# Operand differences as steps of their own, and output-weight sums of three pairs without a trip through DRAM, in attention with two split-fp32 MLPs

## The chip, the cores and the metric

One of the eight cores of a Trainium2 chip runs the kernel. TensorE (PE in the profile) multiplies, with its weight loads shown apart (PEld); VectorE (DVE), ScalarE (ACT) and GpSimd (POOL) work on tiles; SyncE (SP) issues all transfers between DRAM and the on-chip memory. The metric is device microseconds (us) of one execution, the median over several runs.

## What is computed

Attention with a causal window of 128 and a linear position bias, for 4 batches and 8 heads of 576 positions by 64, then two MLPs of 512 to 2048 to 512 over the 2304 positions. The weights of the MLPs reach the chip as 64-bit floats. The reference, cut to what matters:

```python
scores = scale * np.matmul(q, k.transpose(0, 1, 3, 2))
...
attn = attn / (np.sum(attn, axis=-1, keepdims=True) + 1e-09)
x = np.matmul(attn, v)                      # (2304, 512), float32

h = x @ w_in;  r = np.maximum(h, 0.0)       # first MLP
x = (s * (r * r) + b) @ w_out
h = np.maximum(x @ moe2_w_in, 0.0)          # second MLP
out = h * h @ moe2_w_out
```

## The kernel before

**Split products.** Every float32 operand is kept as a high part in the narrow type fp32r and a low part that holds the rest. ACT makes the high part by a copy, DVE the low part by a subtraction (`split`). A product is three matmuls: high by high, high by low, low by high.

**Weights.** A 64-bit word becomes a float32 in steps: a load (token `l`), a first step on ACT and DVE (`a`), a second on ACT or DVE and then POOL or DVE (`b`), and the split into halves (`c`), which are stored to DRAM (`d`) and loaded when they are used (`w`). The words of the second MLP are loaded into three buffers named `st`, for one pair of 128-row blocks of the hidden dimension at a time, eight pairs in all (0 to 7).

**The second MLP's first layer** (phases 0 to 3, each over a quarter of the positions, 32 token numbers in all) uses seven products instead of eight for a 2x2 block product (`p`, 6 matmuls of 128x384 each, out to the PSUM banks `px` and `py`). `m`, `u`, `v` copy partial results to the temps m1, u2, u3 (tiles `tm`, `tu`, `r_all`), `j` adds such a temp to a bank and ACT takes the relu, `r` squares.

**The second MLP's second layer** in phases 0 and 1 is plain (`F`). In phases 2 and 3 it too takes seven products (m = 1, 2, 7, 6, 5, 4, 3, eight steps each, one per pair, so that step number e = 8 times the place of m, plus the pair). Its weight operands are sums and differences of blocks of w_out, which the steps `N` (sums, `second_sums`), `R` (halves) and `t` (stores to `we`) make once for each pair, and which `e` loads (256 KB each) into a ring of places. Its other operand comes from four results of the first layer, a11, a12, a21 and a22: for m = 7 it is a11 - a21, for m = 6 a21 + a22 - a11, for m = 3 a12 - a11, for the others one of the four. `second_operand` (token `g`) makes it: DVE the sum or difference, then ACT the high half, then DVE the low half. `second_product` (token `X`) multiplies, 9 matmuls of 128x256 into the bank `q`. The difference of m = 7 always goes to the one temp u3, which is the tile `r_all`; those of m = 6 and m = 3 overwrite the results (tiles `ywih`, `ywil`, `ywoh`, `ywol`, `yr`). The halves go to a ring of 6 places in phase 2 and 10 in phase 3 (names `m2...`, `sh`, `sl`).

**Output weights and DRAM.** The converted words of w_out of a pair are first split and stored as they are (`c`, `d`). The float words of all but pairs 0 and 1 are stored to DRAM as well (`x`, `store_words`, a transfer `wx<-st`) and come back (`y`, `load_words`, `st<-wx`) much later, when `N`, `R` and `t` make the sums.

**What sets the order.** A list of tokens, `ORDER`, is written out; each token issues its instructions at once, and every engine, and the queue of transfers on SP, executes its instructions in that order. A step that waits holds up everything behind it on its engine. `UNIT_ENGINES` and `CHOICE` say which engine takes the steps that more than one can do (`v` DVE, `g` POOL, `s` ACT). All instructions are issued through one helper, so the profile gives them all line 29 (L29).

Of the kernel before, what the change touches and what calls it, by code (L numbers as in the profile page):

```python
# [18 lines left out]
class InOrder:  # L19
# [20 lines left out]
    T4 a03 a01 c00 b03 b01 C2 U2 D7 X1 S5 c02 X2 X3 L0 i l10 P5 L1 C4 T5 G0 c01 a10 C5 G1 U4 L2 c03 H0 b10 U5 l12 H1 L3  # L40
    l11 D8 X4 D9 G2 G3 M0 X5 M1 H2 M2 a12 H3 S7 l13 a11 S6 c10 L4 b12 L5 b11 P7 P6 M3 T7 T6 c11 C7 C6 G4 U7 U6 L6 G5 c12
    L7 l20 H4 M4 a13 X6 H5 G6 S8 X7 L8 l22 b13 G7 P8 M5 L9 D10 T8 H6 H7 c13 G8 l21 a20 C8 l23 G9 L10 D11 M6 a22 U8 H8 X8
    L11 H9 S9 M7 b20 G10 M8 L12 P9 T9 G11 b22 L13 a21 C9 U9 H10 H11 M9 D12 X9 G12 S10 L14 b21 G13 M10 P10 M11 T10 H12
    H13 c21 L15 c20 M12 c22 C10 U10 G14 a23 H14 X10 l30 G15 M13 L16 S11 M14 b23 L17 G16 P11 D13 L18 T11 H15 c23 M15 H16
    C11 G17 l32 a30 G18 U11 H17 X11 H18 L19 G19 b30 L20 S12 M16 L21 k0.1 a32 l31 M17 M18 P12 T12 a31 H19 G20 c30 C12 H20
    L22 l33 G21 b32 U12 X12 L23 G22 H21 S13 L24 M19 a33 b31 M20 M21 H22 P13 l34 b33 T13 G23 C13 c31 a34 M22 H23 U13 L25
    c33 G24 G25 c32 L26 k3.0 D14 L27 H24 M23 H25 X13 D15 S14 G26 G27 M24 l35 b34 L28 L29 P14 k4.1 T14 M25 H26 a35 C14
    H27 c34 k4.0 G29 b35 U14 M26 D16 X14 G28 H28 S15 L30 c35 P15 M27 M28 T15 C15 D17 G30 L31 H29 G31 U15 X15 L32 S16 M29
    H30 H31 D18 G32 L33 P16 T16 M30 D19 C16 H32 G33 M31 M32 H33 S17 U16 L34 P17 T17 X16 G34 C17 M33 L35 H34 S18 U17 M34
    G35 X17 H35 P18 L36 D20 T18 G36 C18 M35 D21 S19 U18 L37 H36 P19 T19 X18 M36 C19 S20 D22 U19 G37 L38 H37 P20 M37 T20  # L50
    G38 X19 C20 L39 S21 U20 H38 G39 H39 L40 P21 M38 G40 L41 M39 D23 H40 T21 G41 L42 X20 H41 C21 k6.0 S22 U21 M40 k0.0
    P22 T22 X21 C22 M41 S23 U22 G42 D24 H42 k7.0 k1.1 L43 P23 T23 X22 M42 C23 S24 G43 H43 k3.1 U23 P24 L44 T24 D25 D26
    C24 X23 M43 k1.0 G44 H44 L45 G45 S25 U24 L46 D27 M44 k5.0 X24 P25 T25 H45 G46 k2.1 C25 H46 D28 L47 n0.0 n0.1 S26 U25
# [1220 lines left out]
```

## Time and profile before

| | |
|---|---|
| median of the runs (lowest, highest) | 918.45 us (918.18, 919.23) |
| the profiled execution | 916.52 us, of which the span of its trace is 914.7 us |
| PE busy | 878.5 us (96%), granted clock 1.00 from about 59 us on |
| PEld busy | 787.4 us (86%) |
| DVE busy | 663.4 us (73%) |
| ACT busy | 536.7 us (59%) |
| POOL busy | 167.7 us (18%) |
| DMA | 216.8 MB, 237 GB/s over the span |

Busy time is a sum over stages with different limits, so the table alone doesn't say where time can be won; the views by stretch do. A table of stretches gives each engine's busy time in each piece of the span, with the granted clock of TensorE (1.00 is 2.4 GHz, the upper of its two levels), the DMA share and GB/s. A timeline gives the start of a row, its time, engine, line, operation, out<-in, and in brackets the idle time of the engine before it with what ended it. On PE, rows that follow each other undisturbed overlap by some 0.16 us, so the distance of their starts is their price.

### The profile page before, as it was taken

Reading aid. Unit: us, or ns where it says so; the run is one execution under the profiler, and the core shown is the slowest. Engines: PE = TensorE matmul, PEld = TensorE weight load, DVE = VectorE, ACT = ScalarE, POOL = GpSimd, SP = SyncE. Lnnn points to the kernel's source line nnn. Section 1 sums busy time; section 2 is a strip of 40 time slices with the busy share of each in tenths; the row PEclk is TensorE's granted clock in tenths of the full one; section 3 lists DMA queues with packets and bytes.
Section 4 is the critical chain, followed back from the end, with each engine's and each line's share of the span. In section 5 each row is a group of like instructions: output and inputs, shape, how many; then the busy total and the mean of one; then the engine's idle time right before and its main releaser. Section 6 shows DMA issues by size and latency. Waiting matters only on the chain.

```text
span 914.7 us, 16299 instructions
## 1 busy us (share of the span) xinstructions
PE 878.5 (96%) x5680; PEld 787.4 (86%) x5680; DVE 663.4 (73%) x1504; ACT 536.7 (59%) x1227; POOL 167.7 (18%) x242
## 2 busy tenths in 40 slices
PE   5899999999999999989999999999999989999988
PEld 3789998878777777769999998888999989999988
DVE  7998885554558788865565866897969968448775
ACT  7888776454546677754454555666655635446442
POOL 4333221000024454200200122222213200000000
PEclk9899999999999999999999999999999999999999
DMA  9553636126337978988679766887999987876683
GB/s 344 174 190 99 201 112 195 47 70 219 103 100 242 313 248 271 307 305 316 226 287 355 262 229 198 306 294 261 319 336 349 327 282 252 292 265 229 187 271 98
DMA packets 131378, 216.83 MB, mean 237 GB/s; under 512 B 15840, under 2 KB 74208, under 8 KB 131296
## 3 DMA queue, kind: packets, MB, share of 16 engines
q1 hardware_dynamic: 131296, 215.79, 70.0%
q8 instruction: 45, 0.74, 0.3%
q14 instruction: 37, 0.30, 0.1%
HBM read 146.02 MB, written 69.73 MB: 236 GB/s over the span
## 4 chain that ended last, share of the span: by engine, by line
PE 81%; DVE 9%; ACT 4%; DMA 3%; issue 2%; SPq 1%; POOL 0%; ACTq 0%; DVEq 0%
PE ha L29 14%; PE po L29 14%; PE px L29 13%; PE oa L29 12%; PE py L29 10%; PE q L29 8%; PE s L29 7%; PE u L29 2%; DMA m2wol<-wd 1%; DVE ywoh L29 1%; DVE st L29 1%; DVE m2woh L29 1%; DVE pr_t L29 1%; DMA yf<-xd 1%; DMA st<-w_out 1%
## 5 line engine op out<-in xcount | busy, mean ns | idle before, releaser
L29 POOL TENSOR_TENSOR st<-st 128x256 int32<-128x256 int32 (+1 forms) x123 | 87.2, 729 | 363.8 <-DVE st L29 251.0
L29 ACT ACTIVATE pr<-pr,nd 128x256 f32<-128x256 f32 (+1 forms) x125 | 57.9, 474 | 49.5 <-DVE nd L29 49.5
L29 ACT ACTIVATE st<-st 128x512 int32<-128x512 uint32 (+3 forms) x74 | 62.4, 859 | 5.6 <-DVE st L29 3.4
L29 DVE SCALAR_TENSOR_TENSOR r_all<-r_all,s_sb 128x256 f32<-128x256 f32 (+1 forms) x64 | 43.0, 675 | 24.4 <-ACT r_all L29 23.8
L29 ACT ACTIVATE tr<-tr 128x384 f32<-128x384 f32 x48 | 25.2, 525 | 55.4 <-DVE tr L29 55.3
L29 PE MATMUL oa<-ga,woh 128*128 128x256 f32 x256 | 48.2, 287 | 0.0
L29 ACT ACTIVATE r_all<-ha 128x256 f32<-128x256 f32 (+1 forms) x64 | 31.0, 486 | 24.7 <-PE ha L29 19.2
L29 DVE SCALAR_TENSOR_TENSOR st<-st 128x512 int32<-128x512 int32 (+1 forms) x42 | 37.3, 890 | 11.0 <-ACT st L29 10.4
L29 PEld LDWEIGHTS oa<-ga,woh 128*128 128x128 f32 x256 | 39.7, 191 | 2.2 <-issue 1.8
L29 DVE CUSTOM_DVE_ANT_0 pr<-s,bases 128x256 f32<-128x256 f32 (+1 forms) x96 | 31.7, 385 | 11.3 <-PE s L29 11.3
L29 PE MATMUL ha<-x0h,wih 128*128 128x256 f32 x128 | 38.4, 300 | 0.0
L29 PE MATMUL ha<-x0l,wih 128*128 128x256 f32 x128 | 36.6, 286 | 0.0
L29 PE MATMUL ha<-x0h,wil 128*128 128x256 f32 x128 | 36.6, 286 | 0.0
L29 PE MATMUL oa<-ga,wol 128*128 128x256 f32 x128 | 36.2, 283 | 0.0
L29 POOL TENSOR_TENSOR sph<-wih,wil 128x256 f32<-128x256 f32 x17 | 13.5, 814 | 117.7 <-PE ha L29 117.2
L29 ACT ACTIVATE r_all<-px 128x384 f32<-128x384 f32 x32 | 15.7, 490 | 29.5 <-PE px L29 29.4
L29 PE MATMUL s<-raw 64*128 64x256 f32 (+1 forms) x224 | 30.5, 388 | 0.8 <-DVE x0l L29 0.8
L29 DVE TENSOR_SCALAR st<-st 128x512 int32<-128x512 int32 (+2 forms) x52 | 26.2, 507 | 5.9 <-ACT st L29 5.1
L29 POOL TENSOR_TENSOR sph<-sph 128x256 f32<-128x256 f32 x26 | 22.6, 888 | 33.7 <-DVE spl L29 20.9
L29 PE MATMUL px<-m2xl,m2wil 128*128 128x384 f32 x138 | 27.9, 337 | 0.0
L29 PEld LDWEIGHTS ha<-x0h,wih 128*128 128x128 f32 x128 | 24.9, 195 | 3.5 <-issue 2.5
L29 PE MATMUL ha<-x2h,wih 128*128 128x512 f32 x64 | 26.4, 412 | 0.0
(681 smaller groups left out, 2765.9 us busy)
## 6 DMA issues: line engine op xcount, KB each, us to landing
m2wih<-wd SPq DMA_DIRECT2D x19, 512.0 KB, 6.5
st<-w_in SPq DMA_DIRECT2D x8, 1024.0 KB, 6.0
st<-w_out SPq DMA_DIRECT2D x16, 512.0 KB, 5.0
ws<-spl SPq DMA_DIRECT2D x16, 512.0 KB, 4.2
m2wih<-ws SPq DMA_DIRECT2D x16, 512.0 KB, 6.1
wd<-m2wol SPq DMA_DIRECT2D x14, 512.0 KB, 4.5
m2wol<-we SPq DMA_DIRECT2D x26, 256.0 KB, 4.4
st<-w_out SPq DMA_DIRECT2D x6, 1024.0 KB, 6.9
```

The source lines that it names most:

```text
L29: ins = op(*args, **kw)
```

## The change

Three things, in one edit:

1. `second_operand` is cut in two. `parts_of` names the four results and the source; `second_difference` (a new token `q`) issues DVE's sums and differences for m = 7, 6 and 3; `second_operand` (`g`) is left with ACT's copy and DVE's subtraction. The difference for m = 7 goes to u3 and to a new temp u4 in turn.
2. For the pairs in `AT_ONCE` (2, 3 and 4) `second_sums` and the steps behind it read the converted words where they lie (`out_rows`). Their six stores `wx<-st` and six loads `st<-wx`, 256 KB each, are gone, and their `N`, `R` and `t` steps stand beside the conversions of the weights, while phase 0 runs, instead of in phase 2.
3. `ORDER`, `UNIT_ENGINES` and `CHOICE` are new throughout. PE's work is the same in both: 824 product tokens. 15 instructions have left POOL (242 to 227), 18 have come to DVE (1344 to 1362), 2 have left ACT.

```diff
-    D0 S0 D3 P0 S3 D1 l00 l02 P3 S1 T0 P1 T3 T1 a00 D4 D2 l03 C0 a02 b00 U0 X0 b02 S2 S4 C1 U1 C3 U3 P2 P4 T2 l01 D5 D6
...
+    D0 S0 P0 D3 S3 D1 P3 S1 T0 P1 l00 T3 l02 T1 D4 a00 D2 C0 a02 U0 S2 D5 l01 b00 D6 C3 b02 X0 C1 S4 P2 U1 P4 T2 T4 l03
...
-    N1.1:v N2.1:v N3.0:v N3.1:v N7.1:v S0.1:g S1.1:g S2.0:g S3.0:g S3.1:g S4.0:g b0.0:vg b2.2:vg b3.0:vg b3.1:vg
...
+    N0.1:v N1.0:v N3.0:v N4.0:v N4.1:v N5.1:v N6.1:v S0.0:g S0.1:g S1.0:g S1.1:g S3.1:g b0.0:vg b0.2:vg b2.0:vg
...
-EARLY, SOONER = 3, 2
+EARLY, SOONER, AT_ONCE = 3, 2, (2, 3, 4)
...
     def out_rows(k, r, h=0):
-        return raws[(k, r)][:, h * DM:(h + 1) * DM]
+        return raws[(k, r - 2 if r > 3 and k in AT_ONCE else r)][:, h * DM:(h + 1) * DM]
...
-    def second_operand(n, e):
+    def parts_of(n, e):
         m, y = SECOND[e // NP], e % NP
         a11, a22, a12, a21 = (result_of(n * NP + y, c) for c in range(4))
+        return m, a11, a22, a12, a21, {1: a11, 2: a12, 7: temp(f"u{3 + y % 2}"), 6: a11, 5: a21, 4: a22, 3: a12}[m]
+
+    def second_difference(n, e):
+        m, a11, a22, a12, a21, src = parts_of(n, e)
         tt = vector.tensor_tensor
-        src = {1: a11, 2: a12, 7: temp("u3"), 6: a11, 5: a21, 4: a22, 3: a12}[m]
         if m == 7:
             tt(src, a11, a21, ALU.subtract)
         elif m == 6:
             tt(a21, a21, a22, ALU.add)
             tt(a11, a21, a11, ALU.subtract)
         elif m == 3:
             tt(a12, a12, a11, ALU.subtract)
-        split(*operand_halves(n, e), src, act_copy, dve_sub)
+
+    def second_operand(n, e):
+        split(*operand_halves(n, e), parts_of(n, e)[-1], act_copy, dve_sub)
```

**DVE in phase 2's second layer, from m = 7 to m = 6.** `r_all` (u3) and, after the change, `tu_7116` (u4) hold differences of m = 7; rows that write `m2...` or `sl` make low halves; `yw...<-yw...,yw...` are the sums and differences of m = 6. Before:

```order
L29 TENSOR_TENSOR r_all<-ywol_7370,ywoh_7518 128x384
L29 TENSOR_TENSOR m2woh_4705<-r_all,m2woh_4705 128x384
L29 TENSOR_TENSOR ywil_7100<-ywil_7100 128x384
L29 TENSOR_TENSOR ywih_7004<-ywil_7100,ywih_7004 128x384
L29 TENSOR_TENSOR m2wil_4703<-ywih_7004,m2wil_4703 128x384
L29 TENSOR_TENSOR ywoh_7197<-ywoh_7197,ywil_7100 128x384
L29 TENSOR_TENSOR ywil_7100<-ywoh_7197,ywil_7100 128x384
L29 TENSOR_TENSOR m2wil_4703<-ywil_7100,m2wil_4703 128x384
L29 TENSOR_TENSOR ywoh_7286<-ywoh_7286,ywoh_7197 128x384
L29 TENSOR_TENSOR ywoh_7197<-ywoh_7286,ywoh_7197 128x384
L29 TENSOR_TENSOR m2woh_4705<-ywoh_7197,m2woh_4705 128x384
```

After:

```order
L29 TENSOR_TENSOR r_all<-ywoh_7286 128x384
L29 TENSOR_TENSOR tu_7116<-ywol_7372 128x384
L29 TENSOR_TENSOR ywil_7115<-ywil_7115 128x384
L29 TENSOR_TENSOR ywih_7029<-ywil_7115,ywih_7029 128x384
L29 TENSOR_TENSOR m2wil_4702<-r_all,m2wil_4702 128x384
L29 TENSOR_TENSOR m2wih_4462<-ywih_7029,m2wih_4462 128x384
L29 TENSOR_TENSOR m2woh_4723<-tu_7116,m2woh_4723 128x384
L29 TENSOR_TENSOR r_all<-ywol_7372,ywoh_7512 128x384
L29 TENSOR_TENSOR yr_7643<-yr_7643 128x384
L29 TENSOR_TENSOR ob_7909<-q_7685,k2m 128x256
L29 TENSOR_TENSOR tu_7116<-ywoh_7512,yr_7643 128x384
L29 TENSOR_TENSOR m2wil_4702<-ywih_7029,m2wil_4702 128x384
```

Before, each low half (`m2...`) stands directly behind the difference that it is made from. After, three other instructions of DVE lie between the first `r_all` and its low half, four between `tu_7116` and its own, and seven between `ywih_7029` and its own, the last row.

**DVE where the first MLP ends and the second begins.** `ga_63l` is the low half of the first MLP's last operand, which PE waits for; `t1s`, `yt` and `yf` are differences of the second MLP's input, the `m2...` rows their low halves. Before:

```order
L29 TENSOR_TENSOR m2xh_4638<-yf_4571,m2xh_4638 128x768
L29 TENSOR_TENSOR t1s<-yf_4574,yf_4571 128x768
L29 SCALAR_TENSOR_TENSOR ga_63l<-r_all,s_sb,ga_63h 128x512
L29 TENSOR_TENSOR yt_4647<-yf_4592,t1s 128x768
L29 TENSOR_TENSOR m2wih_4650<-t1s,m2wih_4650 128x768
L29 TENSOR_TENSOR yf_4574<-yf_4592,yf_4574 128x768
L29 TENSOR_TENSOR m2xl_4675<-yf_4610,m2xl_4675 128x768
L29 TENSOR_TENSOR m2wol_4678<-yt_4647,m2wol_4678 128x768
```

After:

```order
L29 TENSOR_TENSOR m2xh_4629<-yf_4587,m2xh_4629 128x768
L29 SCALAR_TENSOR_TENSOR ga_63l<-r_all,s_sb,ga_63h 128x512
L29 TENSOR_TENSOR t1s<-yf_4590,yf_4587 128x768
L29 TENSOR_TENSOR yt_4638<-yf_4605,t1s 128x768
L29 TENSOR_TENSOR yf_4590<-yf_4605,yf_4590 128x768
L29 TENSOR_TENSOR m2wih_4653<-t1s,m2wih_4653 128x768
L29 TENSOR_TENSOR m2xl_4656<-yf_4612,m2xl_4656 128x768
L29 TENSOR_TENSOR m2wol_4671<-yt_4638,m2wol_4671 128x768
```

The row of `ga_63l` has moved ahead of `t1s`.

**DVE in phase 2's first layer, token numbers 20 to 22.** Rows `yw...<-py...` take a result out of the bank `py` (the one with `r_all` frees the bank for the next product into it), `yw...<-yw...` square, `m2...<-st...` are low halves of output-weight sums. Before:

```order
L29 TENSOR_TENSOR m2xl_4718<-st_7251,m2xl_4718 128x256
L29 TENSOR_TENSOR ywoh_7286<-py_7231,tu_4701 128x384
L29 TENSOR_TENSOR m2xl_4675<-st_7292,m2xl_4675 128x256
L29 TENSOR_TENSOR ywol_7370<-ywol_7370 128x384
L29 TENSOR_TENSOR ywoh_7286<-ywoh_7286 128x384
L29 TENSOR_TENSOR m2wol_4678<-st_7292,m2wol_4678 128x256
L29 TENSOR_TENSOR ywoh_7286<-ywoh_7286 128x384
L29 TENSOR_TENSOR ywol_7370<-py_7393,tm_4693 128x384
L29 TENSOR_TENSOR ywoh_7197<-ywoh_7197 128x384
L29 TENSOR_TENSOR ywol_7370<-py_7320,r_all 128x384
```

After:

```order
L29 TENSOR_TENSOR ywol_7372<-py_7333,tm_4691 128x384
L29 TENSOR_TENSOR ywoh_7222<-ywoh_7222 128x384
L29 TENSOR_TENSOR ywoh_7286<-ywoh_7286 128x384
L29 TENSOR_TENSOR ywol_7372<-ywol_7372 128x384
L29 TENSOR_TENSOR ywoh_7222<-ywoh_7222 128x384
L29 TENSOR_TENSOR m2wih_4653<-st_7330,m2wih_4653 128x256
L29 TENSOR_TENSOR m2wil_4702<-ywil_7115,m2wil_4702 128x384
L29 TENSOR_TENSOR ywol_7372<-py_7333,r_all 128x384
L29 TENSOR_TENSOR ywoh_7286<-ywoh_7286 128x384
L29 TENSOR_TENSOR st_7348<-st_7348,st_7330 128x256 x2
L29 TENSOR_TENSOR ywol_7372<-py_7419,tm_4691 128x384
L29 TENSOR_TENSOR ywol_7372<-py_7333,tu_4704 128x384
```

The row that adds `r_all` to the bank of number 21 (`py_7320` before, `py_7333` after) has moved ahead of the row of number 22 (`py_7393`, `py_7419`), and one row of weight halves stands in front of it where there were three.

## Rows read from the trace of the kernel before

**Rows 1.** The page, first part: engines over the whole span.

```profile
PE 878.5 (96%) x5680; PEld 787.4 (86%) x5680; DVE 663.4 (73%) x1504; ACT 536.7 (59%) x1227; POOL 167.7 (18%) x242
```

**Rows 2.** Stretches: from:to, length, busy us of each engine (instructions), PEclk, DMA share, GB/s.

```profile
0.00:32.40 32.40, 17.51 (x128) 11.89 (x128) 25.09 (x87) 25.19 (x63) 14.69 (x32) 0.93 0.77 279
...
411.80:713.40 301.60, 299.36 (x1616) 277.14 (x1616) 221.50 (x396) 170.57 (x347) 57.83 (x73) 1.00 0.82 287
713.40:727.50 14.10, 14.10 (x107) 14.03 (x107) 13.47 (x26) 9.47 (x21) 4.80 (x5) 1.00 0.99 356
727.50:769.10 41.60, 37.36 (x278) 35.03 (x277) 30.76 (x63) 17.68 (x40) 0.00 (x0) 1.00 0.83 273
...
865.20:892.00 26.80, 23.37 (x182) 22.03 (x182) 20.61 (x43) 11.38 (x25) 0.00 (x0) 1.00 0.69 232
```

**Rows 3.** Timeline of PE in phase 2, undisturbed second-layer steps.

```profile
769.07 1.24 PE L29 MATMUL q<-m2wih,m2woh 128*128 128x256 f32 x9
770.15 1.24 PE L29 MATMUL q<-m2xh,m2wil 128*128 128x256 f32 x9
```

**Rows 4.** Timeline of PE in phase 2, m = 2, 7 and 6.

```profile
729.44 1.33 PE L29 MATMUL q<-m2wol,m2woh 128*128 128x256 f32 x9 [0.75 <-DMA m2wol<-wd]
...
745.45 1.31 PE L29 MATMUL q<-m2wih,m2woh 128*128 128x256 f32 x9 [1.82 <-ACT m2wih L29]
...
749.38 1.69 PE L29 MATMUL q<-m2wol,m2wil 128*128 128x256 f32 x9 [0.51 <-ACT m2wil L29]
```

**Rows 5.** Timeline of DVE and ACT in phase 2, two operands of m = 6.

```profile
748.13 0.56 DVE L29 TENSOR_TENSOR ywih<-ywil,ywih 128x384 f32<-128x384 f32 x1
...
748.81 0.52 ACT L29 ACTIVATE m2wil<-ywih 128x384 fp32r<-128x384 f32 x1 [1.77 <-DVE ywih L29]
...
749.36 0.56 DVE L29 TENSOR_TENSOR m2wil<-ywih,m2wil 128x384 fp32r<-128x384 f32 x1 [0.67 <-ACT m2wil L29]
...
751.10 0.52 ACT L29 ACTIVATE m2wil<-ywil 128x384 fp32r<-128x384 f32 x1 [1.77 <-DVE ywil L29]
```

**Rows 6.** Timeline of PE in phase 3, m = 7.

```profile
875.42 1.69 PE L29 MATMUL q<-m2wol,m2woh 128*128 128x256 f32 x9 [1.52 <-ACT m2woh L29]
```

**Rows 7.** Timeline of DVE in phase 3, low halves one behind the other.

```profile
889.61 0.55 DVE L29 TENSOR_TENSOR m2wih<-ywih,m2wih 128x384 fp32r<-128x384 f32 x1
890.08 0.55 DVE L29 TENSOR_TENSOR m2wil<-yr,m2wil 128x384 fp32r<-128x384 f32 x1
```

**Rows 8.** Timeline at the seam of the two MLPs.

```profile
397.89 0.51 SPq L29 DMA_DIRECT2D m2wol<-ws  x1
...
399.14 0.96 DVE L29 TENSOR_TENSOR t1s<-yf,yf 128x768 f32<-128x768 f32 x1 [0.85 <-DMA yf<-xd]
...
400.81 0.50 PE L29 MATMUL oa<-ga_63l,woh 128*128 128x512 f32 x1 [2.30 <-DVE ga_63l L29]
```

**Rows 9.** Timeline in phase 2, first layer, numbers 20 to 22.

```profile
701.86 1.20 PE L29 MATMUL py<-m2wih,m2woh 128*128 128x384 f32 x6
...
702.89 1.20 PE L29 MATMUL px<-m2xl,m2xh 128*128 128x384 f32 x6
...
704.34 0.54 DVE L29 TENSOR_TENSOR ywol<-py,r_all 128x384 f32<-128x384 f32 x1
...
704.93 1.33 PE L29 MATMUL py<-m2xh,m2woh 128*128 128x384 f32 x6 [0.84 <-DVE ywol L29]
```

**Rows 10.** Waits of PE over the span: engine, line, releaser: us in total, times, longest.

```profile
PE py L29 <- DVE ywoh L29: 0.8, 1, 0.8
```

**Rows 11.** Timeline of ACT in the first stage.

```profile
30.53 0.66 ACT L29 ACTIVATE x0h<-s 128x256 fp32r<-128x256 f32 x2 [0.95 <-PE s L29]
32.99 0.51 ACT L29 ACTIVATE f_0wih<-f_0wih,nd 128x256 f32<-128x256 f32 x1 [1.80 <-DVE nd L29]
```

**Rows 12.** Transfers: out<-in, queue, count, KB each, median us from issue to landing.

```profile
m2wol<-we SPq DMA_DIRECT2D x26, 256.0 KB, 4.4
...
st<-w_in SPq DMA_DIRECT2D x12, 512.0 KB, 5.1
```

More of the change, by code (lines that the diff above doesn't have):

```diff
@@ L38 @@
 ORDER = """
-    D0 S0 D3 P0 S3 D1 l00 l02 P3 S1 T0 P1 T3 T1 a00 D4 D2 l03 C0 a02 b00 U0 X0 b02 S2 S4 C1 U1 C3 U3 P2 P4 T2 l01 D5 D6
[L40 to L53, printed above, removed]
@@ L144 @@
-    X3.41 X3.42 X3.43 g3.48 X3.44 e3.45 e3.51 e3.48 X3.45 X3.46 O3.5.2 g3.49 X3.48.2 g3.47 X3.49.2 X3.50.2 X3.51.2
-    O3.5.0 g3.53 X3.47 X3.48.0 g3.54 g3.55 X3.49.0 X3.50.0 X3.51.0 O3.4.2 X3.52.0 X3.52.2 X3.53.2 X3.53.0 X3.54.0
-    X3.55.0 X3.54.2 X3.55.2 O3.3.0 O3.3.2 X3.48.1 X3.49.1 X3.50.1 O3.4.0 X3.51.1 X3.52.1 X3.53.1 X3.54.1 X3.55.1 O3.3.1
+    D0 S0 P0 D3 S3 D1 P3 S1 T0 P1 l00 T3 l02 T1 D4 a00 D2 C0 a02 U0 S2 D5 l01 b00 D6 C3 b02 X0 C1 S4 P2 U1 P4 T2 T4 l03
+    a01 c00 a03 b01 C2 c02 X1 U3 U2 S5 X3 X2 L0 i b03 P5 l10 C4 L1 T5 c01 G0 G1 D7 a10 C5 c03 l12 H0 L2 L3 b10 G2 H1 H2
@@ new lines @@
+    X2.19 e2.23 q2.22 X2.20 C2.1.1 e2.33 r23.3 C2.1.0 e2.32 X2.21 O2.2.2 q2.23 e2.27 g2.25 e2.30 e2.28 e2.35 e2.34
+    O2.2.0 m24 X2.24 g2.23 e2.29 g2.22 e2.31 X2.25 q2.26 q2.28 p24.2 X2.22 g2.26 X2.23 g2.27 X2.26 g2.28 C2.7.1 q2.30
+    g2.32 X2.27 q2.29 X2.28 e2.42 X2.32 g2.33 e2.40 g2.30 X2.33 e2.46 g2.29 e2.41 q2.31 g2.34 e2.37 q2.49 C2.7.0 e2.36
+    X2.29 e2.39 X2.30 g2.31 g2.35 X2.34 g2.38 X2.31 e2.38 g2.40 g2.39 g2.36 X2.40 g2.37 X2.35 p24.6 q2.48 V3.5 w27.0
+    e2.43 q2.50 X2.36 X2.37 X2.38 e2.48 e2.54 g2.41 g2.42 e2.47 q2.52 e2.49 g2.43 e2.51 e2.44 q2.54 X2.39 g2.44 X2.41
@@ L157 @@
 CHOICE = dict(x.split(":") for x in """
[L158 to L160 removed]
+    N0.1:v N1.0:v N3.0:v N4.0:v N4.1:v N5.1:v N6.1:v S0.0:g S0.1:g S1.0:g S1.1:g S3.1:g b0.0:vg b0.2:vg b2.0:vg
+    b2.1:vg b3.0:vg b3.1:vg b3.2:vg b3.3:vg b30:vg b33:vg b35:vg b4.1:vg b4.3:vg b5.0:vg b5.1:vg b5.3:vg b6.2:vg
@@ L1219, in attention_mlp2_kernel @@
         for e in range(7 * NP):
-            table.update({f"{x}{n}.{e}": lambda y=y, n=n, e=e: y(n, e) for x, y in (("e", load_second), ("g", second_operand), ("X", second_product))})
+            table.update({f"{x}{n}.{e}": lambda y=y, n=n, e=e: y(n, e) for x, y in (("e", load_second), ("q", second_difference), ("g", second_operand), ("X", second_product))})
             for t in range(3):
```

199 lines of the change are left out of this document (106 added, 93 removed).

## Prediction

> **What bounds the kernel now.** The page's engine line comes first: PE is busy for 878.5 us of a span of 914.7 [rows 1], so 36 us of the span are all that an order can give back, unless PE's own work shrinks, and it doesn't. The table of stretches then says where these 36 us lie [rows 2]: 14.9 in the first 32.4 us, 2.2 in the 302 us from 411.8 to 713.4, 4.2 in the 41.6 us from 727.5 to 769.1 and 3.4 in the 26.8 us from 865.2 to 892.0. The last two are the second layer of phases 2 and 3, from m = 2 to m = 6.
>
> Idle time understates what is lost there, since PE also slows down when it is fed late. I count steps. One X step is 9 matmuls, and undisturbed the next starts 1.08 us later [rows 3]; one p step is 6, and the next starts 1.03 later (the first two of [rows 9]). The stretch of phase 2 holds 278 matmuls, that is 28 X and 4 p steps and two matmuls of its borders [rows 2]: 28 x 1.08 + 4 x 1.03 = 34.4 us of work in 41.6 us, **7.2 us late**. That of phase 3 holds 182, or 20 X steps: 21.6 us of work in 26.8, **5.2 us late**.
>
> The timelines say why. PE waits for high halves from ACT [rows 4, 6]; ACT has waited 1.77 us for a difference from DVE; DVE waits 0.67 us for ACT's copy before it can subtract [rows 5]. The three instructions of one operand follow each other across two engines, and since all stand in one token, DVE begins the next difference only behind the last low half. One operand of m = 6 takes 2.29 us this way (ACT's copies at 748.81 and 751.10) where PE wants one each 1.08. Neither DVE nor ACT is full: in that stretch they are busy for 30.8 and 17.7 of 41.6 us [rows 2]. It is a chain, not a load. Of the 7.2 us of phase 2 about 0.9 is no part of it, a weight that landed late (the first of [rows 4]).
>
> **The change part by part.**
>
> *Differences as own steps, phase 2.* The order of DVE after the change has three to seven other instructions between a difference and its low half, so ACT finds its source ready, copies in 0.52 us, and DVE does other work in the meantime. The chain is gone if DVE's work fits under PE's. After the change DVE has about 60 instructions in this stretch, nearly all of 128x384, beside 31.1 us of PE (fewer p steps lie in it). Back to back such instructions start 0.47 us apart although each shows 0.55 [rows 7]: 60 x 0.47 = 28.2 us, and 28.2 is under 31.1. That this is not too close is shown by the stretch just before: DVE is busy for 13.47 of 14.10 us there, and PE doesn't wait at all [rows 2]. So of the 6.3 us of the chain I take back 5.8: **-5.8 us**. Bounds: -7 if the late weight is early too, -4 if two or three of the sixteen operands of m = 7 and 6 still come late at today's price of about 1 us each [rows 4, 5].
>
> The Trainium skill (VectorE: DVE Perf Modes, section "The DRAIN you can't avoid") speaks against this: after each instruction the next one does not start until the pipe is empty, though it adds that one that is not held starts earlier. By the first half DVE would need 60 x 0.55 = 33 us beside 31.1 of PE; the 0.47 above is the second half, and by that the sum stands. The first half is the rival "DVE full" below.
>
> *The same, phase 3.* 5.2 us late, by the same chain [rows 2, 6]. After: some 45 instructions of DVE, 45 x 0.47 = 21 us, beside 25.8 us of PE: more room than in phase 2. **-4.5 us**, bounds -3 and -5.2.
>
> *Sums of pairs 2 to 4 leave phase 2.* Their POOL, ACT and DVE steps stood between products 16 and 23. PE waits there where DVE frees the bank `py` late: product 21 starts 2.04 us behind its predecessor where 1.03 is the cadence, released by the DVE row of 704.34 [rows 9]; the view of waits has one more like it [rows 10]. In the order after the change this row moves ahead of the next number's and has one row of weight halves before it where it had three. 2 x 1.0 us are at stake, I take **-1.5**, bounds 0 and -2.
>
> *Their transfers.* Twelve transfers of 256 KB go. Those are waited for by POOL, which is off the path (busy for 167.7 of 914.7 us, [rows 1]): cost nothing, gain nothing by themselves. They leave a stretch whose DMA share is 0.99 [rows 2], which helps the weight loads behind them; that is inside the bound of -7 above.
>
> *The seam.* PE waits 2.30 us for `ga_63l`, because DVE does `t1s` first, and that one waited 0.85 for its own data [rows 8]. After, `ga_63l` is ahead. But what comes next on PE needs the weight whose load `m2wol<-ws` was issued at 397.89 [rows 8], and two DVE halves that now stand behind three differences of about 0.9 each. I let most of the 2.3 us be given back there: **-0.5**, bounds -2.3 and +1.
>
> *The first stage.* There ACT and DVE are busy for 25.2 and 25.1 of 32.4 us and PE for 17.5 [rows 2], and they wait for each other. The work ahead of the last first-stage product is the same before and after (by the durations of the trace within 0.3 us on either), but one conversion (b03) goes from before a wait of ACT of 0.95 + 1.80 us [rows 11] into or behind it. It is about 1.1 us of ACT. **-0.8**, bounds -2.5 and +1.5, since this part is ordered anew and its waits cannot be carried over.
>
> *New waits.* In phase 0 the sums of pairs 2 to 4 now stand beside conversions, and a buffer `st` is held until its halves are made. One load is squeezed by it: that of pair 3's first output words is issued behind the halves of pair 2, and 4.5 us of PE work lie before ACT needs it, where such a load takes 5.1 us to land [rows 12]. Behind ACT's waiting step are the relus that PE's banks wait for. That is 0.6 us, and one or two like it are possible. POOL gives sums of some 7 us to DVE, spread over stretches where DVE is busy for 221.5 of 301.6 us [rows 2], so under cover. **+1.0**, bounds 0 and +3.
>
> Sum: -5.8 - 4.5 - 1.5 - 0.5 - 0.8 + 1.0 = -12.1 us. The profiled execution took 916.5 us in all, so 904.4. It lies 1.9 us below the median of 918.45, so the median after is **906.4**.
>
> **The rivals.**
>
> *DVE full.* The chain is replaced by DVE's own rate, as dependent pairs and waits keep it at 0.55 apiece: phase 2 needs 33 us beside 31.1, and the wait for the first operands stays, so about 3 us of the 6.3 remain; phase 3 needs 45 x 0.55 = 24.8 beside 25.8 and keeps perhaps 1.5. That gives back 2.8 + 2.8 of the 10.3: 906.4 + 4.7 = 911. For it: DVE's share in the stretch would be 91% even at 0.47. Against it: 96% without a wait of PE just before [rows 2]. 10 in 100.
>
> *The wait moves to the weights.* Steps at 1.08 us want 256 KB each 1.08 us, besides other traffic: phase 2's stretch moved 273 GB/s x 41.6 us = 11.4 MB, and in 35 us that is 325 GB/s. The stretch before it moved 356 GB/s at a share of 0.99 [rows 2], so it is possible, but a load that takes 4.4 us today [rows 12] takes longer then. If half of the gain of both stretches is given back so, and the rest of the terms come to nothing: 918.45 - 5 = 913. If all of it is, the change doesn't do what it says: 918. 8 in 100 together.
>
> *Slower: the buffers `st`.* There are three. Held until `N` and `R` of pairs 2 to 4 are done, they let the loads of the next words go late, ACT stands at the first conversion step, and with it the relus of phase 0 behind it. The price is a landing of 5.1 us [rows 12] for each load that is issued only when it is wanted. Phase 0 and 1 have 2.2 us of idle PE in 302 today [rows 2], so all of it would be new. It decides from 12.1 + 1.0 + 1.8 = 15 us on, three late loads at full price, one for each pair: 922. Against it: the order keeps 4.5 us of PE work ahead of the tightest of them. 7 in 100.
>
> **How the numbers follow.** Forecast 75 in 100, DVE full 10, weights 8, slower 7. The forecast's own ends, if each term stood at its bound, are 899 and 916; not all will, and 901 to 912 holds most of it. With DVE full (911) and half of the weights case (913) inside, the range is 900 to 914, and what is left out is the slower case, no gain, and the far ends of the forecast, under 2 in 10. A measurement of this kernel can tell about 0.2% from no change, 1.8 us: faster (under 916.6) 0.88, same 0.05, slower (over 920.3) 0.07.
>
> **What would show it.** In the profile after, the two stretches should show X steps at 1.08 us with PE idle under 1 us each, ACT's waits of 1.77 us for `ywih` or `ywil` gone, and DVE's rows at 0.47 to 0.58 without the 0.67 us waits. DVE full shows as rows of DVE without gaps while PE waits for `m2...` from DVE. The weights case shows as PE waiting for a transfer into `m2wol` or its like. The slower case shows as ACT waiting for `st<-w_out` between 430 and 650, with PE behind it. The prediction is wrong if PE's idle time in phase 0 grows by more than the 10.3 us that the two stretches can give.

## The result and the profile after

The changed kernel takes **901.84 us** (median; 901.13 to 902.73) beside 918.32 us (917.83 to 919.23) for the kernel before: a ratio of 0.982, 95% interval 0.9803 to 0.9837, **16.5 us** less. A second comparison, made later, gave 900.76 beside 916.91, ratio 0.9822 (0.9808 to 0.9836). The forecast was 906.4 in a range of 900 to 914, so the sign and the range held and the gain was 4.6 us larger than said.

The profiled execution took 902.73 us (span 900.9), 13.8 less than that of before. The engine line of its page, which answers to [rows 1]:

```profile
PE 876.8 (97%) x5680; PEld 791.6 (88%) x5680; DVE 660.1 (73%) x1522; ACT 531.8 (59%) x1225; POOL 150.4 (17%) x227
```

The 18 instructions that DVE has gained are 1522 against 1504 in these counts.

The stretches of the same places of the order, which answer to [rows 2] (from:to, length, busy us of PE, PEld, DVE, ACT, POOL with instructions, PEclk, DMA share, GB/s):

```profile
414.00:712.40 298.40, 298.40 (x1616) 277.47 (x1615) 223.03 (x415) 166.97 (x343) 47.36 (x64) 1.00 0.82 285
...
725.50:756.80 31.30, 31.30 (x254) 31.28 (x253) 29.16 (x61) 16.33 (x37) 0.00 (x0) 1.00 0.88 296
...
857.20:878.90 21.70, 21.70 (x183) 21.70 (x183) 17.32 (x37) 11.51 (x27) 0.00 (x0) 1.00 0.88 278
```

In each of the three, PE is busy for the whole stretch: 298.40 of 298.40, 31.30 of 31.30, 21.70 of 21.70. Before they had 2.2, 4.2 and 3.4 us of idle time and matmuls that were fed late besides. (The stretch of phase 2 is shorter by itself too: it holds 254 matmuls where it held 278, since one p step and two X steps have moved out of it.) DVE is busy for 29.16 of 31.30 us, 93%.

What has become of one operand of m = 6 in phase 2, from the timeline after (answers to [rows 5]):

```profile
744.46 0.56 DVE L29 TENSOR_TENSOR ywil<-ywoh,ywil 128x384 f32<-128x384 f32 x1
...
744.94 1.14 DVE L29 TENSOR_TENSOR ywoh<-ywoh 128x384 f32<-128x384 f32 x2
745.14 0.53 ACT L29 ACTIVATE m2wil<-ywil 128x384 fp32r<-128x384 f32 x1 [2.21 <-DVE ywil L29]
...
745.57 1.16 ACT L29 ACTIVATE m2woh<-ywoh 128x384 fp32r<-128x384 f32 x2
...
746.00 0.55 DVE L29 TENSOR_TENSOR m2wil<-ywil,m2wil 128x384 fp32r<-128x384 f32 x1
...
747.09 1.24 PE L29 MATMUL q<-m2wih,m2wil 128*128 128x256 f32 x9
...
748.16 1.24 PE L29 MATMUL q<-m2wil,m2woh 128*128 128x256 f32 x9
```

DVE no longer stops between the difference of `ywil` (744.46) and the low half made from it (746.00): it makes the sum and the difference of the next operand meanwhile (744.94, two instructions). ACT makes the high half at 745.14 and goes on with the next two. The two X steps of 9 matmuls start 1.07 us apart. Two signs that the prediction named did not come, though: ACT has waited 2.21 us for `ywil` here, longer than the 1.77 us of before, and in this stretch DVE still waits for ACT three times, 1.1 us at most. PE notices neither, since these operands are made further ahead of their steps.

What PE still waits for after, in the view of waits (engine, line, releaser: us in total, times, longest):

```profile
PE s L29 <- DMA rwih<-first: 4.0, 1, 4.0
PE s L29 <- DVE f_3woh L29: 3.0, 2, 1.7
PE px L29 <- DMA m2wol<-ws: 2.2, 1, 2.2
...
PE px L29 <- ACT tu L29: 0.6, 1, 0.6
PE oa L29 <- DVE ga_63l L29: 0.5, 1, 0.5
```

No row `PE q` is left and none of `py`. All that remains lies in the first stage and at the seam.

### The profile page after: what moved, and what is told of

It reads as the page before. It is cut to its first block, busy times and chain, and to the rows that moved or that the text cites. A ratio compares the mean times of both kernels' runs of the same rounds, so it can differ in the third digit from the quotient of the medians.

```text
span 900.9 us, 16283 instructions
## 1 busy us (share of the span) xinstructions
PE 876.8 (97%) x5680; PEld 791.6 (88%) x5680; DVE 660.1 (73%) x1522; ACT 531.8 (59%) x1225; POOL 150.4 (17%) x227
## 4 chain that ended last, share of the span: by engine, by line
PE 90%; DVE 4%; ACT 3%; DMA 1%; issue 1%; SPq 0%; ACTq 0%; DVEq 0%
PE px L29 15%; PE po L29 15%; PE ha L29 14%; PE q L29 13%; PE oa L29 13%; PE py L29 11%; PE s L29 7%; PE u L29 2%; PE s_t L29 1%; ACT st L29 1%; DMA m2wol<-ws 1%; DVE st L29 1%; DVE pr_t L29 1%; DVE f_0wih L29 0%; PE u_t L29 0%
## 5 line engine op out<-in xcount | busy, mean ns | idle before, releaser
L29 POOL TENSOR_TENSOR st<-st 128x256 int32<-128x256 int32 (+1 forms) x118 | 81.4, 711 | 357.1 <-DVE st L29 234.1
L29 ACT ACTIVATE st<-st 128x512 int32<-128x512 uint32 (+3 forms) x67 | 57.9, 872 | 3.3 <-DVE st L29 3.0
L29 DVE SCALAR_TENSOR_TENSOR r_all<-r_all,s_sb 128x256 f32<-128x256 f32 (+1 forms) x64 | 40.5, 636 | 24.0 <-ACT r_all L29 23.7
L29 ACT ACTIVATE r_all<-ha 128x256 f32<-128x256 f32 (+1 forms) x64 | 30.9, 485 | 29.4 <-PE ha L29 21.7
L29 POOL TENSOR_TENSOR sph<-wih,wil 128x256 f32<-128x256 f32 x14 | 12.4, 897 | 126.0 <-PE ha L29 117.4
L29 DVE TENSOR_SCALAR st<-st 128x512 int32<-128x512 int32 (+3 forms) x59 | 29.1, 493 | 5.8 <-ACT st L29 4.8
L29 PEld LDWEIGHTS s<-raw 64*128 64x128 f32 x224 | 18.6, 191 | 10.1 <-issue 4.6
L29 PE MATMUL ha<-x1h,wih 128*128 128x512 f32 x64 | 26.5, 413 | 0.0
```

Of the source, the lines that this page charges most:

```text
L29: ins = op(*args, **kw)
```

## The experiments

Two theories. **Chain**: the two stretches lost their time because an operand's three instructions followed each other across DVE, ACT and DVE. **Load**: they were helped because the sums, halves and transfers of three pairs have left phase 2. All times below are medians; the kernel before took 916.4 to 917.2 on these chips. Ratios are to the kernel before.

### The chain put back in the changed kernel

```diff
- t7.2 q2.17 X2.9 q2.16 e2.14 g2.13 q2.24 g2.12 X2.10
+ t7.2 X2.9 e2.14 g2.13 g2.12 X2.10
...
- r23.2 g2.17
+ r23.2 q2.17 g2.17
```

and so for all 48 differences.

> The changed kernel with every difference of m = 7, 6 and 3 issued again directly ahead of its own high and low half; nothing else is moved, and the sums of pairs 2 to 4 stay early. Theory (the chain DVE, ACT, DVE of one operand was the loss): X2.9 to X2.40 and X3.24 to X3.40 in the order fall behind by 5 to 8 and 4 to 6 us again, the time goes from 902 to 911 to 915. Rival (load: the stretches were helped because the sums, their halves and transfers of three pairs had left): they stay within 2 us of undisturbed, the time under 905.

Measured: 930.5 us, ratio to before 1.0145 (1.0118 to 1.0172), 28.7 us more than the changed kernel. The stretches, X2.9 to X2.40 and X3.24 to X3.40 in the order:

```profile
725.10:767.90 42.80, 36.05 (x254) 33.31 (x253) 30.16 (x61) 16.52 (x37) 0.00 (x0) 0.96 0.72 246
878.80:905.40 26.60, 25.18 (x180) 23.74 (x181) 20.46 (x42) 12.27 (x28) 0.00 (x0) 0.94 0.70 221
```

They take 42.8 and 26.6 us where they took 31.3 and 21.7: 11.5 and 4.9 us late. The rest of the 28.7 lies around them, above all at m = 3 in phase 2 and in the stretch ahead of X3.24. In phase 2's stretch PE is idle for 6.8 of the 11.5 us; for part of the others it ran slower, at a mean granted clock of 0.96. The chain theory holds, the size was far off: I expected the loss of the kernel before, but the new order seems to lean on the differences. Counted in the order, the halves of m = 7 and 6 in phase 2 stand 2.6 steps of PE ahead of their product after the change and 3.5 before; with the difference it is 6.3. That with the chain back 2.6 steps are too short is the likely reading; no run has varied this distance alone.

The same for m = 7 alone:

```diff
- t7.2 q2.17 X2.9 q2.16 e2.14 g2.13 q2.24 g2.12 X2.10
+ t7.2 X2.9 e2.14 g2.13 q2.16 q2.24 g2.12 X2.10
...
- r23.2 g2.17
+ r23.2 q2.17 g2.17
```

> The changed kernel with only the differences of m = 7 issued directly ahead of their halves; those of m = 6 and 3 stay ahead. Theory: a loss at m = 7 alone; in the trace before, PE fell behind by about 3 us in phase 2 and 3.5 in phase 3 at steps 16 to 23, so 902 to 907 to 909. Rival: m = 7's chain of 1.75 us an operand is hidden by the steps ahead of it once m = 6 is cheap, under 904.

Measured: 906.61 us, ratio 0.9885 (0.9865 to 0.9906): 4.8 us above the changed kernel (6 by the two ratios), just under the expected 907. The stretches take 35.7 and 23.5 us (31.3 and 21.7 after the change): 4.4 and 1.8 us. So m = 7, for which the second temp u4 was made, carries a good part by itself. Whether u4 is needed was not tried apart.

### Each part alone, and both, in the order of before

Differences ahead, nothing else:

```diff
- j23.3 X2.14 g2.17 e2.22 e2.21 g2.15 g2.18 X2.15
+ j23.3 X2.14 q2.18 g2.17 e2.22 e2.21 q2.19 g2.15 g2.18 q2.20 X2.15
```

> The kernel before, in its own order and with all sums of pairs 2 to 7 through DRAM, with one thing of the change: differences are own steps, moved ahead by two to three operands, into u3 and u4 in turn for m = 7. Theory: the 7.2 and 5.2 us of the two stretches go nearly all, 918.3 to 906 to 909. Rival (load): DVE still has the halves of the late sums there, the gain is under 5 us, over 913.

Measured: 909.55 us, ratio 0.992 (0.9902 to 0.9939), 7.7 us gained. The stretches:

```profile
727.80:764.20 36.40, 35.10 (x279) 34.55 (x278) 30.07 (x63) 17.57 (x40) 0.00 (x0) 1.00 0.91 306
860.30:884.80 24.50, 22.43 (x183) 21.84 (x182) 18.89 (x39) 12.54 (x29) 0.00 (x0) 1.00 0.75 253
```

36.4 and 24.5 us, where before took 41.6 and 26.8 for the same 276 and 180 matmuls (the rows count up to three more, at their borders). Of 7.2 and 5.2 us that these were late, 5.2 and 2.3 are gone. What is left there is of another kind, as in this row of PE's timeline (start, us, operation, out<-in, idle time and what ended it):

```profile
744.30 1.31 PE L29 MATMUL q<-m2wih,m2woh 128*128 128x256 f32 x9 [0.79 <-DMA m2wih<-we]
```

PE waits for a weight from DRAM; rows of this kind come to 3.0 us in the run.

The sums of pairs 2 to 4 at once, the chain as it was (for pair 4; pairs 2 and 3 likewise, and three of these sums change between DVE and POOL):

```diff
- b4.3 F10.0 v11 j11.0 F10.6 F10.4 r11.0 p11.4 a5.1 c4.5
+ b4.3 N4.0 F10.0 N4.1 v11 R4.0 j11.0 R4.1 l5.1 F10.6 R4.2 F10.4 R4.3 r11.0 t4.0 p11.4 t4.1 a5.1 t4.2 c4.5 t4.3
```

> The kernel before, in its own order, with the sums of pairs 2, 3 and 4, their halves and stores behind the conversion of the pair, straight from the converted words; no transfers wx<-st and st<-wx for these pairs; differences stay in front of their halves. Theory (the chain is the large part, the sums are a small one): the two bank waits at numbers 20 and 21 and the late weight at X2.10 go, the rest of the two stretches stays 6 and 5 us late: 917.2 to 914 to 917; new waits for buffers st in phase 0 could eat it. Rival (load): the two stretches recover without any change of the chain, under 910.

Measured: 935.25 us, ratio 1.0215 (1.0162 to 1.0268), slower. Two readings. First, the stretches of the chain:

```profile
745.10:786.50 41.40, 38.26 (x278) 36.32 (x277) 30.55 (x63) 17.68 (x40) 0.00 (x0) 0.96 0.80 272
882.60:909.50 26.90, 23.72 (x183) 22.09 (x182) 20.70 (x43) 11.38 (x25) 0.00 (x0) 1.00 0.69 231
```

41.4 and 26.9 us, against 41.6 and 26.8 before. Without the late steps and transfers of three pairs they are as late as with them: **load** has fallen. (A small part can hide: PE is idle for 3.1 us of the first stretch instead of 4.2, but its clock stood at 0.96 instead of 1.00. In the second, at 1.00, nothing was won.) The two bank waits at numbers 20 and 21 are gone, as forecast. Second, the slower rival of the prediction, in the timeline of phase 0:

```profile
596.56 1.23 ACT L29 ACTIVATE st<-st 128x512 int32<-128x512 uint32 x2 [5.67 <-DMA st<-w_in]
...
598.21 1.01 PE L29 MATMUL px<-m2xh,m2wol 128*128 128x384 f32 x2 [8.97 <-ACT tr L29]
```

And PE alone, 100 us earlier:

```profile
500.88 2.26 PE L29 MATMUL px<-m2xl,m2wil 128*128 128x384 f32 x6 [4.83 <-DMA m2wil<-ws]
```

At 596.56 ACT has stood 5.67 us for words in a buffer `st`, and PE 8.97 us for a relu that ACT owes it. The load of these words was issued at 591.11, behind four stores of halves (`we`), and landed 5.4 us later; whether it was late for these stores or for a buffer held too long isn't shown. At 500.88 PE has stood 4.83 us for a weight, which is a place I had not named: the stores `t` of pair 2 now stand ahead of that load in SP's queue. Which of the transfers ahead of it made it late isn't shown. From the first product of number 0 to that of number 16 this kernel takes 263 us, before took 243.

Both parts:

> Both parts in the order of before: differences moved ahead by two to three operands, and the sums of pairs 2 to 4 at once. Theory: the parts add, since in e2_ahead what was left of the two stretches were waits for weights from DRAM (3.0 us), which the missing traffic and steps of three pairs relieve: 909.6 to 903 to 907. Rival (the new order as a whole makes the rest): it stays at 908 or above.

Measured: 928.72 us, ratio 1.0123 (1.0087 to 1.0159). The same two waits in phase 0 stand there, and the stretches take 37.0 and 23.9 us, 36.4 and 24.5 with the differences alone. So the parts add (6.5 us less than the sums alone), but the weights that were late in the run with the differences alone are not relieved by the missing traffic. The expectation missed by the price of my placing. Its rival, 908 or above, came true only in the number, and for that same reason.

### Three rows moved

```diff
- V0.1 T0.1 H63 T0.2
+ V0.1 H63 T0.1 T0.2
...
- p20.5 R3.2 R4.0 w21.3 R3.3 w23.0 v20 t4.0 r18.1 j20.1 r19.3 p20.4
+ p20.5 v20 j20.1 R3.2 R4.0 w21.3 R3.3 w23.0 t4.0 r18.1 r19.3 p20.4
...
- p21.5 j22.0 r19.0 p21.4 j21.1 j21.2 p21.3
+ p21.5 j21.1 j22.0 r19.0 p21.4 j21.2 p21.3
```

> The kernel before with three rows of its order moved: the low half ga_63l ahead of t1s at the seam, and the additions that free the bank py in numbers 20 and 21 ahead of the weight halves and of the next number. Theory: at 694.5 and 702.9 PE no longer waits, -2.0 us; at the seam the wait of 2.3 us for ga_63l goes and most of it comes back as a wait for the first weight, -0.5 us; in all 918.3 to about 916. Rival: the seam gives all of its 2.3 us, 914; or the two bank waits only move to the next product, 918.

Measured: 918.81 us, ratio 1.0014 (1.0003 to 1.0026): nothing won. The waits at numbers 20 and 21 are gone, and this one stands three products behind the first of them:

```profile
702.16 1.14 PE L29 MATMUL py<-m2xl,m2wol 128*128 128x384 f32 x5 [1.71 <-DVE ywoh L29]
```

The addition that frees the bank has become late for another product; DVE's and ACT's work between numbers 16 and 23 is the same. So it was not the place of one row that cost 2 us there: from the first product of number 20 to the first X step the kernel before takes 30.3 us, this one 31.1, and the run with the sums at once 28.4. In that run and in the changed kernel, where that work has left, no such wait is to be found. One of the two comes and goes by itself, though: in the run with the differences alone the wait at 704.9 is missing as well, with all the sums still there, and that stretch takes 30.0 us. The seam gave 0.6 us of its 2.3, near the 0.5 that was expected.

### How much room DVE has

```diff
         if m == 7:
-            tt(src, a11, a21, ALU.subtract)
+            for _ in range(2):
+                tt(src, a11, a21, ALU.subtract)
```

and `range(4)` in the second kernel. Both compute the same difference again.

> The changed kernel with each difference of m = 7 issued twice, the same result both times: 8 more DVE instructions of 128x384 in each of the two stretches. Theory (DVE runs at 0.47 to 0.58 us each and has 2.1 of 31.3 us left in phase 2 and 4.4 of 21.7 in phase 3): 8 x 0.5 = 4 us don't quite fit in phase 2, +1 to +2.5 us, and fit in phase 3. Rival (DVE has room, since its order allows much more slip): no change. Rival (DVE is already the bound): +8 us.

> The same with three more of each, 24 more instructions in each stretch: 24 x 0.5 = 12 us of DVE. Theory: less the room of 2.1 and 4.4 us, +10 and +7.5 us, 901.8 to 919. If the instructions that write the same tile one behind the other start 0.58 us apart, +12 and +9.5, 923.

Measured: 907.41 and 926.43 us, 5.6 and 24.6 above the changed kernel (6.6 and 24.8 by the ratios, 0.9892 and 1.009), both more than expected. The stretch of phase 2 with 8 repeats in it, and with 24:

```profile
725.50:760.30 34.80, 32.14 (x255) 31.44 (x254) 33.22 (x69) 16.44 (x37) 0.00 (x0) 1.00 0.82 271
```

```profile
724.00:770.00 46.00, 37.07 (x252) 36.05 (x253) 42.58 (x85) 16.27 (x37) 0.00 (x0) 0.89 0.63 203
```

The timeline of DVE with 24:

```profile
744.02 2.33 DVE L29 TENSOR_TENSOR tu<-ywol 128x384 f32<-128x384 f32 x4
746.27 0.55 DVE L29 TENSOR_TENSOR ywil<-ywil 128x384 f32<-128x384 f32 x1
...
747.33 0.55 DVE L29 TENSOR_TENSOR m2wil<-r_all,m2wil 128x384 fp32r<-128x384 f32 x1
747.80 0.55 DVE L29 TENSOR_TENSOR m2wih<-ywih,m2wih 128x384 fp32r<-128x384 f32 x1
```

The four subtractions into one tile take 2.33 us; less the 0.55 of the last one, their starts lie 0.59 us apart ((2.33 - 0.55) / 3). The row behind them, into another tile, starts 0.47 after the last of them, and the two low halves start 0.47 apart. Eight repeats are then 8 x 0.59 = 4.7 us of DVE and cost 3.5 us in phase 2's stretch (34.8 for 31.3), so there was room for about **1.2 us** (an estimate), not the 2.1 that the expectation took from the 29.16 of 31.30 us above. In phase 3 they cost the rest of the 5.6, about 2.1 us, so some 2.6 us were free there. With 24 repeats, 14.2 us of DVE, phase 2's stretch is 14.7 us longer (46.0 for 31.3), more than the 13.0 that the same room would leave; PE idles there for 8.9 us and its mean clock is 0.89. "DVE full", the first rival, was close by: it would have begun with two or three instructions more.

The Trainium skill (VectorE: DVE Perf Modes, section "The DRAIN you can't avoid") says both that the next instruction waits for the pipe to empty and that one that is not held starts earlier. This trace shows 0.59 us a piece into the same tile and 0.47 into different ones, beside a shown duration of 0.55. So the sum that rested on 0.47 was the right one for this stretch (61 rows at 0.47 are 28.7 us, and 29.16 are shown busy); what it left free was less than it seemed.

### Two tries to go further

In the run with the differences alone, 36 loads of weights moved up:

```diff
- g2.32 e2.32 X2.23 q2.30 g2.33 C2.7.0 e2.33 X2.28 g2.29 X2.32 e2.36 q2.31
+ g2.32 X2.23 q2.30 g2.33 C2.7.0 X2.28 g2.29 e2.36 X2.32 q2.31
```

(`e2.32`, `e2.33` and others now stand further up.)

> e2_ahead (order of before, differences ahead) with 36 loads of second-layer weights moved up to 21 steps of the order earlier, as far as their places in the ring are free, so that they stand about 7 products ahead instead of 0 to 5. Theory: what e2_ahead had left in the two stretches, 3.0 us of PE waiting for m2wol<-we and m2wih<-we, were loads placed for the slow chain of before; they go, 909.6 to 906 to 907.5, and the stretches come to 35 and 22.5 us. Rival (the transfers themselves are the limit there, at a DMA share of 0.83 and more): the waits move to other loads and the time stays at 909 to 910.

Measured: 914.28 us, ratio 0.9968 (0.9954 to 0.9983), worse than the 909.55 without. Phase 3 did as expected (22.8 us for 24.5), phase 2 lost 6.3 us (42.7 for 36.4):

```profile
729.50:772.20 42.70, 38.58 (x279) 37.34 (x278) 29.73 (x62) 17.11 (x40) 0.00 (x0) 0.92 0.80 262
868.30:891.10 22.80, 22.12 (x182) 21.71 (x181) 18.82 (x39) 12.47 (x29) 0.00 (x0) 1.00 0.76 260
```

PE's timeline in the first of them:

```profile
746.86 1.30 PE L29 MATMUL q<-m2wih,m2wil 128*128 128x256 f32 x9 [0.82 <-DMA m2wih<-we]
750.07 2.26 PE L29 MATMUL q<-m2wih,m2woh 128*128 128x256 f32 x9 [1.90 <-DMA m2wih<-we]
```

In phase 2 the stores `t` of the late pairs stand in the same queue. The loads that PE waits for here, those of X2.20 and X2.21, are not among the moved ones; that the moved ones pushed them back is the likely reading, not shown. Of the 6.3 us PE is idle for 2.8 more than without (4.1 for 1.3), and the clock's mean is 0.92 where it was 1.00. The waits moved to other loads in phase 2, as the rival says, and went in phase 3, as the theory says; neither foresaw a loss.

In the changed kernel, the first weight of the second MLP ahead of the input's loads:

```diff
- X39 Q L63 Y0.0 Y0.1 M61 Y0.3 H62 Y0.2 w0.0 n7.5 w0.1
+ X39 w0.0 Q L63 Y0.0 Y0.1 M61 Y0.3 H62 Y0.2 n7.5 w0.1
```

> The changed kernel with one transfer earlier: the first weight of the second MLP (m2wol<-ws, behind which PE waited 2.2 us) is issued ahead of the eight loads of its input instead of behind them; its buffer has been free since 392.5 us and the queue idle until 395.3. Theory: the first product starts at 403.7 instead of 406.1, then the next wait is for the halves of t2, which end at 407.8 against a start of that product at 408.3; so about 1 us of the 2.4 stays won, 901.8 to 900.8. Rival: the loads of the input come later by the transfer's 1.3 us and nothing is won.

Measured: 900.5 us, and the changed kernel on the same chip 900.76: not to be told apart. PE starts the first product with no wait (404.67) and then waits for halves instead:

```profile
404.67 1.23 PE L29 MATMUL px<-m2xh,m2wol 128*128 128x384 f32 x6
406.38 0.44 PE L29 MATMUL py<-m2xl,m2wol 128*128 128x384 f32 x1 [0.49 <-ACT m2xl L29]
407.37 1.15 PE L29 MATMUL py<-m2xl,m2wol 128*128 128x384 f32 x5 [0.55 <-DVE m2xl L29]
```

### The first stage once more

> The changed kernel once more, on one chip with the run below and with the kernel before. Expected: 901 to 903 against 916 to 918. For the first stage: the granted clock between 32 and 58 us was 0.89 in four profiles and 0.93 to 1.00 in six, of both orders; where it is 0.95 or more the step L6 should begin before 60 us, else after 61.

Measured: 900.76 us, and a clock of 0.89 between 32 and 58.3 us with the step L6 at 61.6, as that rule said. Another profile doesn't obey it: the run with three rows moved had 0.93 there and L6 at 59.6. Of thirteen profiles, seven had 0.93 to 1.00 there and L6 at 58.3 to 59.6, six had 0.89 and L6 at 61.1 to 62.1. The tables of stretches of the changed kernel and, behind it, of the one with m = 7 put back show how it comes about:

```profile
54.00:56.00 2.00, 0.17 (x2) 0.17 (x3) 1.89 (x6) 2.00 (x8) 1.52 (x3) 1.00 0.14 54
56.00:58.00 2.00, 2.00 (x13) 2.00 (x13) 2.00 (x5) 1.80 (x3) 0.00 (x0) 0.63 0.00 0
58.00:60.00 2.00, 2.00 (x17) 1.67 (x17) 1.36 (x4) 1.95 (x4) 0.00 (x0) 0.51 0.04 8
```

```profile
54.00:56.00 2.00, 0.20 (x2) 0.20 (x3) 1.82 (x6) 2.00 (x8) 0.87 (x2) 1.00 0.00 0
56.00:58.00 2.00, 2.00 (x22) 1.83 (x22) 2.00 (x6) 2.00 (x4) 0.00 (x0) 1.00 0.00 0
58.00:60.00 2.00, 2.00 (x35) 1.83 (x30) 1.58 (x5) 2.00 (x5) 0.00 (x0) 1.00 0.03 8
```

The first stage of these two kernels is the same. In both PE idles for some 2 us around 54 to 56 us, waiting for the probabilities that it is to transpose. In the first the granted clock then is 0.63 and 0.51, that is near the lower level of 1.2 GHz, for 4 us; in the second it stays at 1.00. L6 begins at 61.24 and 59.59. The kernel with both parts in the order of before, whose first stage is that of the kernel before, fell to 0.63 and 0.51 as well and has L6 at 61.7; the kernel before had 1.00 and 58.9. The wait ahead of the transposes and L6, in the kernel before and, behind it, in the changed one:

```profile
55.13 1.97 PE L29 MATMUL s<-ident,f_3woh 128*128 128x128 f32 x16 [1.71 <-ACT f_3woh L29]
...
58.92 0.39 PE L29 MATMUL ha<-x0h,wih 128*128 128x256 f32 x1
```

```profile
55.83 3.04 PE L29 MATMUL s<-ident,f_3woh 128*128 128x128 f32 x16 [1.86 <-ACT f_3woh L29]
...
61.24 0.39 PE L29 MATMUL ha<-x0h,wih 128*128 128x256 f32 x1
```

What decides between the two isn't settled: a wait of 1.86 us was followed by a fall and one of 2.33 was not. But the order may have a share in it. Five of the seven profiles with the changed first stage fell, and one of the six with that of before. The six that fell had waited 1.86 to 2.34 us at this place, six of the seven others 1.51 to 1.75, and the seventh 2.33.

## Why the prediction was right, point by point

By the trace of one execution each, 13.8 us lie between the kernels, and 12.1 were said.

| step | said | found | |
|---|---|---|---|
| differences ahead, phase 2 | -5.8 | -7.2 | all of what was late, the late weight included |
| the same, phase 3 | -4.5 | -5.2 | all of what was late |
| bank waits, numbers 20 to 22 | -1.5 | -2.0 | both gone |
| the seam | -0.5 | -0.3 | `ga_63l` waits 0.55 us, the first weight 2.19 |
| the first stage | -0.8 | +2.3 | 0.7 ahead of the fall of the clock, 1.6 behind it |
| new waits in phase 0 | +1.0 | -0.8 | none came, an old one went |

The rest, about 0.6 us, is spread. The seam went as said; of the rows that answer to [rows 8], on PE and on SP's queue,

```profile
401.08 0.50 PE L29 MATMUL oa<-ga_63l,woh 128*128 128x512 f32 x1 [0.55 <-DVE ga_63l L29]
...
406.09 1.31 PE L29 MATMUL px<-m2xh,m2wol 128*128 128x384 f32 x6 [2.19 <-DMA m2wol<-ws]
```

```profile
399.29 0.94 SPq L29 DMA_DIRECT2D m2wol<-ws  x2
```

the weight is issued at 399.29 and PE starts on it at 406.09.

**Phases 2 and 3.** The mechanism was right and shown from both sides: put back, the chain costs 4.8 us for m = 7 alone and more than it had cost before for all; given to the kernel before, its removal gains 7.7. What I held back (1.4 and 0.7 us) was not needed. Given alone it gives 7.5 of the 12.4 in the two stretches; in the order of before, loads of weights are then late. That they are not in the changed kernel is the new order's work. How much of that is the order of the loads and how much the emptier queue isn't shown: my two attempts at either failed. The rival of the weights said that a load of 4.4 us would take longer at the higher rate; in the profile after, `m2wol<-we` takes 4.2 us in the median, with 296 GB/s in phase 2's stretch.

**The bank waits.** Right in the result, and better founded than I said: the prediction read them as a matter of two rows' places. The run with three rows moved shows that moving rows only hands the wait on; that the sums had left was what mattered, since with them gone the waits go in the old order too. That one of the two can also be missing with the sums in place makes the share of each, about 1 us, uncertain.

**New waits.** The rival's price is real: in the old order with my own placing, late words and a late weight cost about 20 us. It was underestimated too: PE stood 8.97 us for one late load of words, not 5.1, and a weight came late as well. The order of the changed kernel avoids it; the one load I took for squeezed caused no wait of PE. The old wait that went, 0.8 us for a relu at 567, stands beside another at 582 in other profiles of the same order of phase 0 (waits of 2.3 and 2.2 us in all in the runs with three rows moved and with the differences alone); no profile with the order of the changed kernel has either.

**The first stage.** The step that failed. The transposes begin 0.7 us later than before, at 55.83 for 55.13, where 0.8 less was said; then the clock falls, and L6 is 2.3 us later. I read ACT's work and waits and left the clock out, although the first 32.4 us stood at 0.93 in [rows 2]. Where the clock kept 1.00 there, L6 came at 58.3 and 59.6 with the new first stage and at 58.7 to 59.6 with the old: the 0.8 us are not to be seen in these either, and what moving b03 gave isn't shown.

**From the profile to the median.** Of the 4.6 us between forecast and result, 1.7 are the sum and 2.8 this: the profiled execution of before lay 1.8 to 1.9 us below its median, and I took the same for the one after. That one lay 0.9 above its median, being one of those that fell to the lower clock. The six profiled executions that fell all lie above the median of their runs, by 0.8 to 2.7 us; the seven others lie between 1.9 below and 1.3 above. An offset between one execution and a median belongs to that execution and is not to be carried over.

**Slips in the working.** None of them decides anything. The four stretches it lists hold 24.7 of the 36 us. The 2.2 us of idle PE that it gives to phases 0 and 1 contain the two bank waits of phase 2 (0.80 and 0.84). By its own parts, 3 of 6.3 and 1.5 of 5.2 us remaining as loss, "DVE full" comes to 909.7 and not 911. With each term at its upper bound the forecast ends at 917, not 916. Phase 3's stretch came out as 37 rows of DVE beside 21.7 us, where 45 beside 25.8 were said.

## What to carry to other kernels

Where two engines take turns on one operand, count the time of a full turn against what the consumer wants per step: idle time of both engines beside a waiting consumer points to a chain, and it is cut by issuing the first step of the next operands ahead, with a second temp where they share one. Moving work away doesn't cut such a chain, and moving one row doesn't remove a wait that comes from the amount of work. In an order built on the cut, taking it back cost 28.7 us where giving it to the old order had gained 7.7, and a part of a change moved into another order can cost more than it gives, as the sums did here.

## What the runs showed of the hardware that was not expected

- TensorE's granted clock fell after some waits of 2 to 3 us within a stretch, and made them dearer. With 24 repeats the stretch of 46.0 us ran at a mean of 0.89; in pieces of 2 us, PE is idle in one of them (a wait of 3.1 us in all) and the clock is at 0.50, 1.2 GHz, soon after:

```profile
728.00:730.00 2.00, 0.00 (x0) 0.00 (x0) 1.93 (x5) 1.17 (x4) 0.00 (x0) 1.00 1.02 363
730.00:732.00 2.00, 1.17 (x7) 1.17 (x8) 2.00 (x5) 0.25 (x1) 0.00 (x0) 0.85 0.70 263
732.00:734.00 2.00, 2.00 (x12) 2.00 (x11) 2.00 (x6) 0.69 (x2) 0.00 (x0) 0.50 0.36 135
...
736.00:738.00 2.00, 2.00 (x18) 2.00 (x17) 1.93 (x4) 0.53 (x1) 0.00 (x0) 1.00 0.92 304
```

  The kernel before had 4.2 us of idle PE in its stretch, 1.82 at the longest, and kept 1.00.
- Between runs of the same first stage the same wait is sometimes followed by 4 us at the lower level and sometimes not; that is 1.7 to 3 us by the step L6, as much as a measurement of this kernel tells from no change.
- DVE's subtractions of 128x384 start 0.59 us apart into one tile and 0.47 into different ones, both shown as 0.55 to 0.56 long.
